# Two layers of long convolution and gated MLP on one core: copies, order of rows, late sums and turned rows in a planned instruction stream

## The chip, the cores and the metric

The kernel runs on one core of a Trainium2 chip. The core has a matrix engine (TensorE, PE in the profile; its weight loads are PEld), a vector engine (VectorE, DVE), an activation engine (ScalarE, ACT), a general engine (GpSimd, POOL) and a queue engine (SyncE, SP) that only issues DMAs here. Each takes its own instructions in order; they wait for one another through semaphores. SBUF is the working memory. PSUM is the small memory into which TensorE writes its products. The metric is the device time of one execution in microseconds; lower is better.

## The reference

All data are bfloat16 with S = 2048 tokens, D = 576 and F = 4608. Two layers with the same weights follow each other, each of them a convolution gate A and an MLP B, both with a residual and a layer norm in front:

```python
kv = k_shift * v                          # k_shift: causal 4-tap filter of k
y  = irfft(rfft(kv) * rfft(ssm_k))[:S]    # convolution of length S along the tokens
y  = y + kv * ssm_D
A(q) = q * y
B(x) = (gelu(x @ w_gate) * (x @ w_up)) @ w_down

x = q
x = x + A(layernorm(x)); x = x + B(layernorm(x))
x = x + A(layernorm(x)); x = x + B(layernorm(x))
```

The convolution's result y depends on k, v and the filter alone, not on x, so both layers use the same y.

## The kernel before

**Tiling.** The 2048 tokens are four chunks c of 512, each four rows j of 128 tokens (RT = 4). A unit is one layer on one chunk; the eight units are, in order, (0,0), (0,1), (1,0), (1,1), (0,2), (0,3), (1,2), (1,3), numbered 0 to 7. They are done in the passes [0], [1,2], [3,4], [5,6], [7]. F is cut into three phases (NP = 3) of 12 column tiles (FP = 12). A visit is one unit in one phase, and within a pass the phases are the outer loop, so that two units share the streamed weights: 24 visits.

**A visit.** For each of 12 column tiles fi, `gu` (L834) makes the gate and the up product in one PSUM slot "gu", 18 matmuls. ScalarE takes the gelu of the gate half (L1317, ga), and VectorE multiplies it with the up half out of PSUM (L1318, hT). Then for each row j 24 matmuls (L1330, dn) make the down product in a slot "dn". VectorE adds it to the residual x_c: L1365 in the first phase, L1367 in the second, L1359 in the third for layer 0, and for layer 1 the third writes the output tile ob (L1350), which a DMA stores. The slots of gu and dn come from `pr` (L607), which goes round three PSUM slots. A fourth slot is that of the convolution, cps. In the down products the convolution may also take a slot of the three (`conv.alt`).

**Rows of a unit.** Before a unit's first visit each of its rows is gated with the convolution (ScalarE yh at L731, VectorE x_c at L741), its mean and variance are found (POOL L692, ScalarE square at L700, POOL L707 and L708), it is normalised to bf16 (VectorE xn at L770 and L772) and turned, so that features lie on partitions, by two DMA transposes issued from SP (`spread`, L798) into xnT. These steps lie in two lists: `vq` for VectorE (in order) and `aq` for ScalarE (by priority). There is one yh tile, four xn tiles and two ob tiles.

**The convolution.** It works by chunks (`Conv.step`): filter kv (VectorE L253, L259, L265), forward products of kv and of the filter (TensorE L285, ScalarE eo at L288, VectorE L293), products of spectra (VectorE L301, L304, L305) summed over chunks in f32 tiles ac (L476), sums and differences (L313, L318), and four inverse products (TensorE L328, ScalarE copy into y at L330). Chunk 0 is done in the prologue (0 to some 50 us). Chunk m = 1 is done beside unit 0's three visits and is needed by unit 1, which follows them. Spectra of earlier chunks are kept in DRAM and come back as kr and hr by DMAs that POOL issues (L391, L395).

**What sets the order.** The program is written out engine by engine in the order in which the Python code emits it. A small model of time, `Pace` (fields pe, dve, act), is advanced by constants (C_GU = 1.944 us for a column tile, C_DN, C_HT and so on). After each tile and within the down products `fill` (L866) is called with a limit: it issues loads that are due, and puts out VectorE work from the convolution (`run_v`) or from the rows (`run_vq`) as long as the model's VectorE stays below the limit, then at most one ScalarE task (`run_aq`), and, where `tensor` is true, up to three pieces of convolution on TensorE (`run_p`). In the up/gate stage the limit lies LEAD = 1.8 us past the next tile, and `tensor` is true while `hurry()` holds, that is until the last inverse product of chunk 1 has been put out. `conv_first` (while chunk 1 has VectorE work left) puts the convolution ahead of the rows. `pressing` says that the unit due next still has rows to make; then the convolution's VectorE work is held back.

Of the kernel before, what the change touches and what calls it, by code (L numbers as in the profile page):

```python
# [18 lines left out]
P = 128  # L19
# [4 lines left out]
HW = 288  # L24
# [11 lines left out]
C_TT, C_ST, C_BN, C_NORM, C_HT, C_GELU, C_EVA, C_EVD, C_YH = 0.76, 0.82, 0.47, 0.62, 0.69, 0.6, 0.66, 0.76, 0.8  # L36
LAG = 0.25
AHEAD = 2.0
HOLD, LEAD = 14.0, 1.8
# [91 lines left out]
class Conv:  # L131
# [9 lines left out]
    def __init__(self, tc, ctx, pace, A_k, A_v, A_shift_k, A_ssm_k, A_ssm_D, ident, cps, ypool):  # L141
        self.tc, self.nc, self.t = tc, tc.nc, pace
        self.k2, self.v2, self.hk = A_k[0], A_v[0], A_ssm_k
        self.S, self.D = self.k2.shape
        self.NB = self.S // BS
        self.KS = A_shift_k.shape[1]
        self.sk, self.sD = A_shift_k, A_ssm_D
        self.ident, self.cps, self.ypool = ident, cps, ypool
        D = self.D
        pool = lambda name, bufs: ctx.enter_context(tc.tile_pool(name=name, bufs=bufs))  # L150
        self.cst = pool("c_cst", 1)
        self.krp = pool("c_kr", 3)
# [17 lines left out]
        self.y_at = {(0, j): 0.0 for j in range(RT)}  # L170
        self.kv_at, self.fwd_at, self.hf_at, self.hd_at = {}, {}, {}, {}
# [149 lines left out]
    def inverse(self, m, mt, terms):  # L321
# [8 lines left out]
        nc.scalar.activation(out=self.halves(self.y[m][:, mt, :]), in_=ps[:, :, 0:HW], func=ACT.Copy)  # L330
# [4 lines left out]
    def store(self, dst, t, ready):  # L335
        self.spills.append((ready, lambda: self.nc.gpsimd.dma_start(out=dst, in_=t[:])))
# [5 lines left out]
    def step(self, m, kv=None, loaded=False):  # L342
# [115 lines left out]
        def v(kt, a, part):  # L458
            def run():
                K = kc[kt] if a == m else kr[(kt, a)][1]  # L460
                if a == 0:
                    acc[kt, part] = self.acp.tile([P, D], F32, tag="ac", name="ac")
                prs[part] = self.prod(part, K, hr[(kt, a)][1], acc[kt, part][:] if a == 0 else None)
# [9 lines left out]
        def more(kt, part):  # L473
            def run():
                into = acc[kt, part][:]
# [12 lines left out]
        def shift(kt, part):  # L488
            def run():
                for sg in range(2):  # L490
                    prev = self.yb[(1 - part, kt, sg)]
                    self.shifted(nyb[part, kt, sg], prev, part)
                    z[(part, kt, sg)] = prev
                return lambda when: mark(("z", kt, part), when + LAG)
            return run
        now = lambda: 0.0
        for kt in KTS:
            order = [(a, part) for a in range(m + 1) for part in range(2)]
            for a, part in order if kt < 2 else sorted(order, key=lambda k: k[1]):
                keys = [("ld", kt, a)] + ([("kc", kt % 2, s, h) for s in range(2) for h in range(2)] if a == m else [])  # L500
                self.V.append((get(*keys), C_P1 if part else C_P0, v(kt, a, part)))
                if a > 0:
                    self.V.append((now, C_AC, more(kt, part)))
# [12 lines left out]
        def inv(mt):  # L516
            def run():
                self.yb = nyb
                self.inverse(m, mt, [(self.lhs(kt, s, mt), z[(s, kt, mt % 2)])
                                     for kt in range(2) for s in range(2)])  # L520
                done = t.on_act(C_EVA, t.pe + 0.98 + LAG)
# [45 lines left out]
def ssm_geglu_kernel(ctx, tc, A_q, A_k, A_v, A_shift_k, A_ssm_k, A_ssm_D, B_x, B_w_gate, B_w_up,  # L567
# [38 lines left out]

    def pr(name):  # L607
        taken[0] += 1
# [7 lines left out]
    gwork = pool("gwork", 1)  # L616
# [5 lines left out]
                lambda: bank(turn[3], "cps"), ypool)  # L622
# [54 lines left out]
    def sum_task(c, j, v):  # L677
# [5 lines left out]
        aq.append((2, lambda: xb_at.get(c, NEVER), C_SQ, run))  # L683
# [12 lines left out]
    def square_task(get_x, v):  # L696
# [14 lines left out]
        aq.append((0 if v["pfx"] == "l_" else 2, at_v(v, "nm_at"), C_SQ, run))  # L711

    def run_aq(limit):
        found = [(prio, n) for n, (prio, ready, cost, run) in enumerate(aq) if ready() <= t.pe]
# [3 lines left out]
        _, _, cost, run = aq[n]  # L718
# [6 lines left out]
    def gate_task(c, j, g):  # L725
        def ready():
            return NEVER if gates[0] is not g else max(conv.y_at.get((c, j), NEVER), g.get("rstd_at", NEVER))
# [6 lines left out]
        aq.append((1, ready, C_YH, run))  # L734
# [19 lines left out]
    def act_early(c):  # L754
        gvars[c] = [{"pfx": "e_"} for _ in range(RT)]
# [7 lines left out]
    def prep(ui, j):  # L763
        layer, c = units[ui]
        v = nvars.setdefault(ui, [{"pfx": "l_"} for _ in range(RT)])

        def norm(j):
            def run():
                xn = xnp.tile([P, XW], BF16, tag="xn", name="xn")
# [3 lines left out]
                xn_made.append((ui, j, xn, t.dve + C_NORM + 0.3))  # L773
# [13 lines left out]
    def g_sum(c, j):  # L787

        v = hvars.setdefault(c, {})[j] = {"pfx": "g_"}
# [3 lines left out]
    xn_made = deque()  # L793

# [14 lines left out]
    def run_vq(limit):  # L809
# [7 lines left out]
        else:  # L817
            r = NEVER if len(xn_made) >= 3 else need[1].get("rstd_at", NEVER)
# [21 lines left out]
    def gu_half(pair, fi, n):  # L840
        gu(pair, wgu[fi // FG], fi % FG, lambda a: a.rearrange("p (j q) -> p j q", q=P)[:, n::2, :], xnT_of[0])

# [18 lines left out]
    def pressing():  # L861

        ui = coming[0]
        return ui is not None and xn_done.get(ui, 0) < RT and (units[ui][1], 0) in conv.y_at and bool(vq)

    def fill(limit, tensor, conv_first):  # L866
        weights()
        conv.run_loads()
        spreads()
        while True:  # L870
            if conv_first:
# [5 lines left out]
        if tensor:  # L877
            for _ in range(3):
                if not conv.run_p():
# [11 lines left out]
    with tc.manual_schedule():  # L891
# [7 lines left out]
        with ExitStack() as es:  # L899
# [257 lines left out]
            for j in (0, 2, 1, 3):  # L1157
# [42 lines left out]
                def norm(j=j):  # L1200
                    v = vs0[j]
                    xn = held["xn", j] = xnp.tile([P, XW], BF16, tag="xn", name="xn")
# [73 lines left out]
        for n, (wb, ph, ui, first, final) in enumerate(visits):  # L1276
            coming[0] = next((v[2] for v in visits[n + 1:] if v[2] != ui), None)
            layer, c = units[ui]
            while xn_done.get(ui, 0) < RT:
                if not run_vq(t.pe + 3.0):  # L1280
                    conv.run_loads()
                    run_aq(t.pe + 3.0)
                    conv.run_v(t.pe + 1.5)
                    conv.run_p()
                    t.pe += 0.2
                spreads()
# [13 lines left out]
            end = ph == NP - 1  # L1300
            hT = hpool.tile([P, FP, CH], BF16, tag="hT", name="hT")
            free = deque([0.0] * 3)
            conv.alt = None
            for fi in range(FP):
# [11 lines left out]
                ga = work.tile([P, CH], F32, tag="ga", name="ga")  # L1316
                nc.scalar.activation(out=ga[:], in_=pair[:, 0, :], func=ACT.Gelu_apprx_tanh)  # L1317
                nc.vector.tensor_tensor(out=hT[:, fi, :], in0=ga[:], in1=pair[:, 1, :], op=ALU.mult)  # L1318
                free.append(t.on_dve(C_HT, t.on_act(C_GELU, t.pe + 0.15) + 0.15) + 0.1)
                if gi == FG - 1 and final:  # L1320
                    when_due(t.pe + (FP - FG) * C_GU + 12.0, load_wgu, n + 3)
                fill(t.pe + C_GU + LEAD, hurry(), conv.left > 0)
            for j in range(RT):
# [24 lines left out]
                if layer == 1 and end:  # L1348
                    ob = work.tile([P, D], BF16, tag="ob", name="ob")
                    nc.vector.tensor_tensor(out=ob[:].rearrange("p (h d) -> p h d", h=2), in0=xh,  # L1350
                                            in1=acc[:, :, 0:HW], op=ALU.add)
                    dst = out2[c * CH:(c + 1) * CH, :].rearrange("(p j) d -> p j d", j=RT)[:, j, :]
                    if wb == NWB - 1:
                        nc.sync.dma_start(out=dst, in_=ob[:])
                    else:
                        conv.store(dst, ob, t.pe + 0.2 + C_EVD + LAG)
                elif end:
                    v = g_sum(c, j)
                    nc.vector.scalar_tensor_tensor(out=xh, in0=acc[:, :, 0:HW], scalar=1.0, in1=xh, op0=ALU.mult,  # L1359
                                                   op1=ALU.add, accum_out=v["s"][:])  # L1360
                    mean_after(v, t.pe + 0.2 + C_EVD + LAG)
                    square_task(lambda xa=xa: xa, v)
                elif ph == 0:
                    m_, op = shift.pop((c, j))
                    nc.vector.scalar_tensor_tensor(out=xh, in0=acc[:, :, 0:HW], scalar=m_[:, 0:1], in1=xh, op0=op, op1=ALU.add)  # L1365
                else:
                    nc.vector.tensor_tensor(out=xh, in0=xh, in1=acc[:, :, 0:HW], op=ALU.add)  # L1367
                t.on_dve(C_EVD, t.pe + 0.2)
                if layer == 0 and end:
                    vq.extend(prep(units.index((1, c)), j))  # L1370
# [51 lines left out]
```

## Time and profile before

The median of three runs is 960.4 us (960.04 to 961.02). The profile is of another execution.

| what | value |
|---|---|
| time of the profiled execution | 961.26 us |
| its span, first to last instruction | 959.5 us |
| mean granted TensorE clock | 0.993 |
| TensorE busy | 931.6 us, 97% |
| VectorE busy | 562.7 us, 59% |
| ScalarE busy | 312.8 us, 33% |
| POOL busy | 139.0 us, 14% |
| gu matmuls, L837 | 561.2 us |
| dn matmuls, L1330 | 292.8 us |
| gelu, L1317, 285 of them | 598 ns each |
| hT, L1318, 285 of them | 686 ns each |
| first term of a sum, f32 (L305, ac<-prod), 24 of them | 758 ns each |
| later terms of it in bf16 (L305, prod<-prod), 48 of them | 458 ns each |

How to read the lines shown later: in the table by stretch each engine has its busy time and, in brackets, its instructions; then follow the granted clock (1.00 is full speed), the mean busy share of the DMA engines and GB/s. A line of the timeline has start, length, engine, line of the program, operation, tile written <- tiles read, shape, count, and in square brackets the idle time of the engine before it with what ended it. In the chain, the steps are those that the end of the program hung on.

### The profile page before, as it was taken

How to read it: one execution, taken by the hardware profiler on the slowest of the kernel's cores; microseconds unless marked ns; L12 is line 12 of the kernel's file. 1: busy time of each engine (PE TensorE's matmuls, PEld its weight loads, DVE VectorE, ACT ScalarE, POOL GpSimd, SP SyncE). 2: the span in 40 equal slices, each digit the busy share in tenths (PEclk: the TensorE clock that was granted, in tenths of full speed). 3: DMA queues.
4: the chain of work that ended last, by engine and by line, in shares of the span. 5: the costliest groups of instructions: out<-in, count | busy, mean ns of one | idle time of the engine just before them, and what ended most of it. 6: DMA issues, size and time to landing. Idle time of an engine off the chain costs nothing.

```text
span 959.5 us, 19259 instructions
## 1 busy us (share of the span) xinstructions
PE 931.6 (97%) x8198; PEld 540.0 (56%) x8198; DVE 562.7 (59%) x1030; ACT 312.8 (33%) x560; POOL 139.0 (14%) x302
## 2 busy tenths in 40 slices
PE   8999999499999999999999999999999999999998
PEld 5756466255646656556466465466466456456455
DVE  7768886367988965677899723543333324423332
ACT  5654214351322335433211521552211214411211
POOL 2214101312211203222020200230000002100000
PEclk9999999799999999999999999999999999999999
DMA  9999986726843722893591540483540540596730
GB/s 236 182 282 266 270 246 120 173 51 177 197 154 120 139 75 83 192 234 76 113 282 40 99 125 14 87 172 78 99 124 1 101 123 11 93 234 148 152 71 25
DMA packets 128970, 131.02 MB, mean 137 GB/s; under 512 B 43378, under 2 KB 121075, under 8 KB 128884
## 3 DMA queue, kind: packets, MB, share of 16 engines
q1 hardware_dynamic: 119554, 93.34, 45.7%
q0 software_dynamic: 9200, 35.54, 11.7%
q8 instruction: 64, 1.05, 0.5%
q10 hardware_dynamic: 130, 0.90, 0.3%
q14 instruction: 22, 0.18, 0.1%
HBM read 108.53 MB, written 11.80 MB: 125 GB/s over the span
## 4 chain that ended last, share of the span: by engine, by line
PE 92%; DMA 2%; issue 2%; DVE 1%; ACT 1%; POOL 0%; SPq 0%; DVEq 0%; ACTq 0%; POOLq 0%
PE gu L837 57%; PE dn L1330 27%; PE cps L285 2%; PE ps L276 2%; PE cps L328 1%; DMA out_dram<-ob 1%; DMA xnT<-xn 1%; PE ps L837 1%; DMA k<-in_A_k_dram 1%; PE ps L1015 1%; PE ps L1121 1%; PE ps L1047 0%; PE ps L1142 0%; ACT yh L731 0%; DVE x_c L741 0%
## 5 line engine op out<-in xcount | busy, mean ns | idle before, releaser
L837 PE MATMUL gu<-xnT,wgu 64*128 64x512 bf16 x5130 | 561.2, 377 | 8.4 <-DMA xnT<-xn 7.4
L837 PEld LDWEIGHTS <-wgu 64*128 64x128 bf16 x5238 | 256.7, 94 | 313.6 <-issue 20.4
L1317 ACT ACTIVATE ga<-gu 128x512 f32<-128x512 f32 x285 | 170.3, 598 | 538.9 <-PE gu L837 535.1
L1318 DVE TENSOR_TENSOR hT<-ga,gu 128x512 bf16<-128x512 f32 x285 | 195.5, 686 | 246.8 <-ACT ga L1317 246.3
L1330 PE MATMUL dn<-wd,hT 128*128 128x288 bf16 x2304 | 292.8, 286 | 0.5 <-DVE ob L1339 0.5
L1330 PEld LDWEIGHTS <-hT 128*128 128x128 bf16 x2304 | 223.5, 98 | 66.5 <-issue 10.5
L1367 DVE TENSOR_TENSOR x_c<-x_c,dn 128x576 f32<-128x576 f32 x32 | 24.1, 753 | 39.1 <-PE dn L1330 38.9
L692 POOL TENSOR_SCALAR means<-s 128x1 f32<-128x1 f32 x28 | 9.4, 336 | 227.7 <-DVE x_c L1359 193.8
L288 ACT ACTIVATE eo<-cps 128x576 f32<-128x576 f32 x48 | 30.5, 649 | 24.4 <-PE cps L285 17.1
L1365 DVE SCALAR_TENSOR_TENSOR x_c<-dn,means,x_c 128x576 f32<-128x576 f32 x28 | 22.8, 815 | 24.8 <-PE dn L1330 24.8
L476 DVE TENSOR_TENSOR ac<-ac,prod 128x576 f32<-128x576 f32 x48 | 36.2, 754 | 0.7
L708 POOL TENSOR_TENSOR rstd<-ve,neghalf_t 128x1 f32<-128x1 f32 x56 | 35.5, 634 | 4.7
L391 POOL DMA_DIRECT2D kr<-Kd x24 | 13.3, 552 | 100.3 <-DVE prod L304 100.3
L1350 DVE TENSOR_TENSOR ob<-x_c,dn 128x576 bf16<-128x576 f32 x15 | 11.3, 753 | 27.9 <-PE dn L1330 19.3
L731 ACT ACTIVATE yh<-y,rstd 128x576 f32<-128x576 bf16 x28 | 21.6, 772 | 14.0 <-DVE x_c L741 11.5
L395 POOL DMA_DIRECT2D hr<-Hd x36 | 19.5, 543 | 45.2 <-DVE prod L304 45.1
L305 DVE TENSOR_TENSOR prod<-prod 128x576 bf16<-128x576 bf16 x48 | 22.0, 458 | 1.7
L1359 DVE SCALAR_TENSOR_TENSOR x_c<-dn,x_c 128x576 f32<-128x576 f32 x16 | 12.1, 757 | 17.5 <-PE dn L1330 16.6
L700 ACT ACTIVATE junk<-x_c,nm 128x576 bf16<-128x576 f32 x28 | 21.5, 768 | 1.3 <-POOL nm L692 1.3
L293 DVE TENSOR_TENSOR kc<-eo 128x288 bf16<-128x288 f32 x48 | 19.3, 453 | 4.2 <-ACT eo L288 3.8
L707 POOL TENSOR_SCALAR ve<-ss 128x1 f32<-128x1 f32 x56 | 15.4, 275 | 38.0 <-ACT junk L700 37.5
L293 DVE TENSOR_TENSOR hh<-eo 128x288 bf16<-128x288 f32 x48 | 19.3, 452 | 2.3 <-ACT eo L288 2.2
(139 smaller groups left out, 539.6 us busy)
## 6 DMA issues: line engine op xcount, KB each, us to landing
wgu<-in_B_w_gate_dram SPq DMA_DIRECT2D x45, 576.0 KB, 5.7
wd<-in_B_w_down_dram SPq DMA_DIRECT2D x30, 864.0 KB, 7.7
wgu<-in_B_w_up_dram SPq DMA_DIRECT2D x45, 512.0 KB, 7.6
hr<-Hd POOLq DMA_DIRECT2D x36, 288.0 KB, 5.6
kr<-Kd POOLq DMA_DIRECT2D x24, 288.0 KB, 5.2
Kd<-kc POOLq DMA_DIRECT2D x12, 288.0 KB, 6.2
Hd<-hh POOLq DMA_DIRECT2D x12, 288.0 KB, 4.2
k<-in_A_k_dram POOLq DMA_DIRECT2D x3, 1008.0 KB, 9.6
```

The lines of the kernel that those rows point to most:

```text
L288: nc.scalar.activation(out=eo[:], in_=ps[:, :, 0:HW], func=ACT.Copy, scale=scale)
L293: self.nc.vector.tensor_tensor(out=dst, in0=eo[:, 0, :], in1=eo[:, 1, :], op=op)
L305: nc.vector.tensor_tensor(out=dst, in0=pr[:, 0, :], in1=pr[:, 1, :], op=ALU.subtract if part == 0 else ALU.add)
L476: nc.vector.tensor_tensor(out=into, in0=into, in1=prs[part], op=ALU.add)
L708: nc.gpsimd.tensor_tensor(out=v["rstd"][:], in0=ve[:], in1=neghalf_t[:, 0:1], op=ALU.pow)
L731: nc.scalar.activation(out=g["yh"][:], in_=conv.y[c][:, j, :], func=ACT.Identity, scale=g["rstd"][:, 0:1], bias=1.0)
L837: nc.tensor.matmul(cols(pair[:, s, :]), lhsT=w[r0:r0 + HK, k, gi * P:(gi + 1) * P], rhs=cols(xnT[r0:r0 + HK, blk_of[k], :]), start=(k == 0 ...
L1317: nc.scalar.activation(out=ga[:], in_=pair[:, 0, :], func=ACT.Gelu_apprx_tanh)
L1318: nc.vector.tensor_tensor(out=hT[:, fi, :], in0=ga[:], in1=pair[:, 1, :], op=ALU.mult)
L1330: nc.tensor.matmul(acc[:, h, 0:HW], lhsT=hT[:, fi, j * P:(j + 1) * P], rhs=wd[2 * wb + fi // WT][:, fi % WT, h * HW:(h + 1) * HW], start=( ...
L1365: nc.vector.scalar_tensor_tensor(out=xh, in0=acc[:, :, 0:HW], scalar=m_[:, 0:1], in1=xh, op0=op, op1=ALU.add)
L1367: nc.vector.tensor_tensor(out=xh, in0=xh, in1=acc[:, :, 0:HW], op=ALU.add)
```

## The change

It has five parts.

- **Copies by ScalarE in the first visits.** While `hurry()` holds, and if the model's ScalarE is not behind, ScalarE takes the gelu into bf16 and then copies the up half out of PSUM into bf16 too, and VectorE multiplies the two from SBUF. The PSUM slot is free after the copy. `fill` may then work FAR = 3.6 us past the next tile.
- **First terms of the convolution's sums stay bf16**, and the second term makes the f32 sum from two bf16 products.
- **Rows of the unit that is due go first.** `pressing` holds from the moment when VectorE has finished the chunk's spectra. While it holds, `run_aq` takes tasks of that unit alone, and TensorE gets no further convolution work once that chunk's y is there. Gating has priority over squares and has two yh tiles. The inverse's copy goes to VectorE if ScalarE is behind it.
- **Down sums put out when ready.** The sum of a down product is not put out right behind it. It goes into a list `late`; `fill` puts it out first thing when the model says that it is ready, and `pr` does at the latest before its slot comes round. Sums that make the output (ob) are put out at once as before. The ob tiles now come from the four xn tiles, in one ring with the rows.
- **Last rows turned by TensorE.** Rows that are finished in the last SLOW = 6 us of the visit before, or are missing when their visit is to begin, are turned by nine TensorE transposes into the cps slot and copied out by VectorE or ScalarE (`turn_row`).

```diff
+SLOW = 6.0
+HOLD, LEAD, FAR = 14.0, 1.8, 3.6
...
-                prs[part] = self.prod(part, K, hr[(kt, a)][1], acc[kt, part][:] if a == 0 else None)
+                prs[part, a] = self.prod(part, K, hr[(kt, a)][1])
...
-                nc.vector.tensor_tensor(out=into, in0=into, in1=prs[part], op=ALU.add)
+                nc.vector.tensor_tensor(out=into, in0=prs[part, 0] if a == 1 else into, in1=prs[part, a], op=ALU.add)
...
+                if max(t.dve, t.pe + 0.98) < max(t.act, t.pe + 0.98):
+                    nc.vector.tensor_copy(out=out, in_=in_)
...
+    def run_late(limit):
+        if not late or late[0][0] > t.pe or max(t.dve, t.pe - 1.0) + C_EVD > limit:
+            return False
+        ready, _, run = late.popleft()
+        run()
+        t.on_dve(C_EVD, ready)
+        return True
...
     def pr(name):
+        while late and taken[0] - late[0][1] >= 2:
+            ready, _, run = late.popleft()
+            run()
+            t.on_dve(C_EVD, ready)
         taken[0] += 1
...
-    gwork = pool("gwork", 1)
+    gwork = pool("gwork", 2)
...
     def run_aq(limit):
-        found = [(prio, n) for n, (prio, ready, cost, run) in enumerate(aq) if ready() <= t.pe]
+        only = coming[0] if pressing() else None
+        found = [(prio, n) for n, (prio, ready, cost, run, ui) in enumerate(aq) if (only is None or ui == only) and ready() <= t.pe]
...
+    ring = deque(maxlen=4)
...
+    def out_tile():
+        if not xn_open():
+            spreads(True)
+            conv.flush(NEVER)
+        return xn_tile()
...
-    def spreads():
-        while xn_made and xn_made[0][3] <= t.pe:
-            ui, j, xn, _ = xn_made.popleft()
+    def spreads(now=False, tensor=False):
+        while xn_made and (now or xn_made[0][3] <= t.pe):
+            if tensor and xn_made[0][0] == ahead[1] and t.pe > ahead[0] - SLOW and conv.ps_free[0] <= t.pe:
+                turn_row(*xn_made.popleft())
+                continue
...
+    def turn_row(ui, j, xn, when, entry):
...
+        pt = conv.cps((P, 2, 1024), BF16)
+        for b in range(NKC):
+            c0 = b * P if b < 5 else HK + (b - 5) * P
+            nc.tensor.transpose(pt[:, b // 8, (b % 8) * P:(b % 8 + 1) * P], xn[:, c0:c0 + P], ident[:])
...
+        if max(t.dve, t.pe) <= max(t.act, t.pe) + 0.3:
+            nc.vector.tensor_copy(out=dst, in_=src)
...
+        else:
+            nc.scalar.copy(out=dst, in_=src)
...
     def pressing():
-        return ui is not None and xn_done.get(ui, 0) < RT and (units[ui][1], 0) in conv.y_at and bool(vq)
+        return ui is not None and xn_done.get(ui, 0) < RT and units[ui][1] in conv.z_at and bool(vq)
...
     def fill(limit, tensor, conv_first):
         weights()
         conv.run_loads()
-        spreads()
+        spreads(tensor=tensor)
         while True:
+            if run_late(limit):
+                continue
...
             for _ in range(3):
-                if not conv.run_p():
+                if pressing() and (units[coming[0]][1], RT - 1) in conv.y_at or not conv.run_p():
                     break
...
             while xn_done.get(ui, 0) < RT:
-                if not run_vq(t.pe + 3.0):
+                if xn_made and xn_made[0][3] - 0.3 <= t.pe:
+                    turn_row(*xn_made.popleft())
+                elif not run_late(t.pe + 3.0) and not run_vq(t.pe + 3.0):
...
-                ga = work.tile([P, CH], F32, tag="ga", name="ga")
-                nc.scalar.activation(out=ga[:], in_=pair[:, 0, :], func=ACT.Gelu_apprx_tanh)
-                nc.vector.tensor_tensor(out=hT[:, fi, :], in0=ga[:], in1=pair[:, 1, :], op=ALU.mult)
-                free.append(t.on_dve(C_HT, t.on_act(C_GELU, t.pe + 0.15) + 0.15) + 0.1)
+                if hurry() and t.act <= t.pe + 0.2:
+                    ga = work.tile([P, 2, CH], BF16, tag="ga", name="ga")
+                    nc.scalar.activation(out=ga[:, 0, :], in_=pair[:, 0, :], func=ACT.Gelu_apprx_tanh)
+                    nc.scalar.copy(out=ga[:, 1, :], in_=pair[:, 1, :])
+                    nc.vector.tensor_tensor(out=hT[:, fi, :], in0=ga[:, 0, :], in1=ga[:, 1, :], op=ALU.mult)
+                    there = t.on_act(2 * C_GELU, max(t.pe + 0.15, gone[0]))
+                    gone.append(t.on_dve(C_HB, there + 0.15) + 0.1)
+                    free.append(there + 0.1)
+                    lead = FAR
+                else:
+                    ga = work.tile([P, CH], F32, tag="ga", name="ga")
+                    nc.scalar.activation(out=ga[:], in_=pair[:, 0, :], func=ACT.Gelu_apprx_tanh)
+                    nc.vector.tensor_tensor(out=hT[:, fi, :], in0=ga[:], in1=pair[:, 1, :], op=ALU.mult)
+                    gone.append(t.on_dve(C_HT, t.on_act(C_GELU, max(t.pe + 0.15, gone[0])) + 0.15) + 0.1)
+                    free.append(gone[-1])
+                    lead = LEAD
...
-                fill(t.pe + C_GU + LEAD, hurry(), conv.left > 0)
+                fill(t.pe + C_GU + lead, hurry(), conv.left > 0)
...
-                    ob = work.tile([P, D], BF16, tag="ob", name="ob")
+                    ob, entry = out_tile()
...
-                elif end:
...
-                t.on_dve(C_EVD, t.pe + 0.2)
...
+                else:
+                    def plus(c=c, j=j, layer=layer, ph=ph, end=end, acc=acc, xa=xa, xh=xh):
...
+                    late.append((t.pe + 0.2, taken[0], plus))
```

More of the change, by code (lines that the diff above doesn't have):

```diff
@@ L329, in inverse, with store, run @@
                                  start=(n == 0), stop=(n == len(terms) - 1))
-        nc.scalar.activation(out=self.halves(self.y[m][:, mt, :]), in_=ps[:, :, 0:HW], func=ACT.Copy)
+        return self.halves(self.y[m][:, mt, :]), ps[:, :, 0:HW]
     def spill(self, dst, t, ready=0.0):
         self.spills.append((ready, lambda: self.nc.gpsimd.dma_start(out=dst, in_=t[:].rearrange("p s d -> p (s d)"))))
-    def store(self, dst, t, ready):
-        self.spills.append((ready, lambda: self.nc.gpsimd.dma_start(out=dst, in_=t[:])))
+    def store(self, dst, t, ready, entry):
+        def run():
+            self.nc.gpsimd.dma_start(out=dst, in_=t[:, 0:self.D])
+            entry[0] = True
+        self.spills.append((ready, run))
     def flush(self, now, keep=0):
@@ L502, in step @@
                 if a > 0:
-                    self.V.append((now, C_AC, more(kt, part)))
+                    self.V.append((now, C_AC, more(kt, part, a)))
                 if kt >= 2 and a == m:
@@ L518, in run @@
                 self.yb = nyb
-                self.inverse(m, mt, [(self.lhs(kt, s, mt), z[(s, kt, mt % 2)])
-                                     for kt in range(2) for s in range(2)])
-                done = t.on_act(C_EVA, t.pe + 0.98 + LAG)
+                out, in_ = self.inverse(m, mt, [(self.lhs(kt, s, mt), z[(s, kt, mt % 2)])
+                                                for kt in range(2) for s in range(2)])
+                if max(t.dve, t.pe + 0.98) < max(t.act, t.pe + 0.98):
+                    nc.vector.tensor_copy(out=out, in_=in_)
+                    done = t.on_dve(C_EVD, t.pe + 0.98 + LAG)
+                else:
+                    nc.scalar.activation(out=out, in_=in_, func=ACT.Copy)
+                    done = t.on_act(C_EVA, t.pe + 0.98 + LAG)
                 self.ps_free[self.cur] = done + LAG
@@ L717, in run_aq @@
         n = min(found)[1]
-        _, _, cost, run = aq[n]
+        cost, run = aq[n][2:4]
         if max(t.act, t.pe - 1.0) + cost > limit:
@@ L754, in act_early @@
     def act_early(c):
-        gvars[c] = [{"pfx": "e_"} for _ in range(RT)]
+        gvars[c] = [{"pfx": "e_", "ui": units.index((0, c))} for _ in range(RT)]
         for j in range(RT):
```

113 lines of the change are left out of this document (75 added, 38 removed).

## The prediction

> **What bounds the kernel now.** I read the page first, then the chain of work in order of time, the table by stretch, the waits, and last the timeline around single places.
>
> ```profile
> span 959.5 us, 19259 instructions
> PE 931.6 (97%) x8198; PEld 540.0 (56%) x8198; DVE 562.7 (59%) x1030; ACT 312.8 (33%) x560; POOL 139.0 (14%) x302
> ```
>
> TensorE is busy for 931.6 of 959.5 us, so only the 27.9 us in which it stands, and its slow clock, can be won; work taken off another engine counts only where TensorE waits for it. The chain in order of time (start, length, what) shows where that is:
>
> ```profile
> 131.04 23.42 PE gu L837 x216
> ...
> 178.57 1.27 SPq L798
> 179.93 7.11 DMA xnT<-xn
> 187.08 25.87 PE gu L837 x216
> ```
>
> An undisturbed visit has 23.42 us of up/gate products (12 groups of 1.952) and 11.87 us of down products. The visit at 187.08, the first of unit 1, starts only when the last rows of its input, turned by DMA, have landed, and its products take 25.87 us. The table by stretch (length, then busy time by engine, then granted clock) gives the size of the hole and what leads to it:
>
> ```profile
> 98.40:156.50 58.10, 58.10 (x524) 30.59 (x519) 52.74 (x93) 13.80 (x24) 3.74 (x7) 1.00 0.89 226
> 172.10:187.10 15.00, 2.74 (x18) 1.53 (x16) 6.78 (x20) 6.84 (x14) 6.82 (x14) 0.70 0.77 164
> 187.10:213.00 25.90, 25.90 (x217) 12.83 (x217) 13.40 (x29) 11.04 (x22) 3.83 (x11) 0.91 0.45 105
> ```
>
> From 98.4 to 156.5 VectorE is busy 52.74 of 58.10 us with the convolution of chunk 1; then come its inverse products (157.5), the rows of unit 1, and the hole: 2.74 us of TensorE work in 15.00 us, clock 0.70, then 0.91. ScalarE has 13.80 of 58.10 us in use. The waits (who for whom: total, times, longest) name the rest:
>
> ```profile
> PE gu L837 <- DMA xnT<-xn: 7.4, 1, 7.4
> PE cps L285 <- ACT eo L288: 5.2, 3, 2.5
> PE gu L837 <- DVE ob L1350: 1.0, 1, 1.0
> ```
>
> 4.8 us of the 5.2 lie inside the hole (gaps of 2.3 and 2.5 us before 175.34 and 178.52). The third line is small, but it tells of the PSUM ring, and so does an ordinary boundary in the timeline:
>
> ```profile
> 671.83 6.43 PE L837 MATMUL gu<-xnT,wgu 64*128 64x512 bf16 x58
> 671.93 0.82 DVE L1365 SCALAR_TENSOR_TENSOR x_c<-dn,means,x_c 128x576 f32<-128x576 f32 x1 [2.12 <-PE dn L1330]
> 673.98 0.60 ACT L1317 ACTIVATE ga<-gu 128x512 f32<-128x512 f32 x1 [13.32 <-PE gu L837]
> 674.61 0.69 DVE L1318 TENSOR_TENSOR hT<-ga,gu 128x512 bf16<-128x512 f32 x1 [1.86 <-ACT ga L1317]
> ...
> 852.49 0.75 DVE L1350 TENSOR_TENSOR ob<-x_c,dn 128x576 bf16<-128x576 f32 x1 [2.69 <-DMA out_dram<-ob]
> ...
> 853.30 4.92 PE L837 MATMUL gu<-xnT,wgu 64*128 64x512 bf16 x44 [1.00 <-DVE ob L1350]
> ```
>
> At 853.30 the third group of a visit waited for the last down sum of the visit before: the sum ended at 853.24 (852.49 + 0.75), the products went on 0.06 later. Three PSUM slots go round, so the third group needs the slot of the last down row.
>
> **The change, part by part.** Sums are against the profiled execution's own time, 961.26 us (span 959.5); the median is 960.4, 0.9 less.
>
> *The hole (gain).* Of its 15.00 us four convolution groups of 0.49 us (L285) must be done anyway: 15.0 - 1.96 = 13.0 us. The slow clock costs 25.87 - 23.42 = 2.45 more. Full gain: 15.5 us. Whether it goes depends on when chunk 1 is ready. From 98.4 to 156.5 VectorE does 24 products hT at 0.684 us. With both operands copied down as bf16, I price one by the nearest row, 0.458 us for a 576-wide bf16 product with bf16 output; scaled to 512, 0.41. 24 x 0.27 = 6.6 us. The first term of each sum now stays bf16: 8 x (0.758 - 0.458) = 2.4 us. VectorE stood 5.4 us in this stretch, nearly all (5.7 by that line's idle time) before products waiting for ScalarE; with 3.6 us of work allowed ahead instead of 1.8 I take half away, 2.7. So 156.5 becomes about 145, even if the stretch starts no earlier. Before, it took 2.3 us to the first y copy (158.77) and 20.2 from there to the last xn row (178.36 + 0.57); at the same pace that row is there at about 167.5, while TensorE is busy until about 171. Rows of the due unit go first now, so the pace should be better. By DMA the fourth row landed 8 us after its xn (187.08), which would be 175.5; on TensorE it takes 0.56 + 0.76 us (next item), 169. Between no gain (rows as late as before) and 15.5 us it is nearest to the latter: I take 15.5.
>
> The cover for this is ScalarE: a copy of about 0.60 us (the gelu row, same shape) in each of up to 36 groups, 21.6 us. In 98.4 to 156.5 that raises 13.8 by 14.4 to 28 of 58 us. Each group then holds ScalarE 1.2 of 1.952 us, so the copies are hidden; in the first visit, with convolution copies of 0.65 and sums of 0.87 to 0.96 between them, ScalarE's clock in the planner passes over some. Without that cover each late copy would cost TensorE up to 0.6 us.
>
> *Turned rows (loss).* One row is 9 transposes. In the prologue a set of 8 plus 2 halves took about 0.56 us of TensorE (first matmul 50.24, next set 50.81), the copy 0.76 on VectorE or 1.12 on ScalarE, hidden where the row is not the last. Only rows finished in the last 6 us of a visit, or missing at its start, go this way. Before, only unit 1 is that late: unit 3's transposes ended 16 us before use, unit 7's 11 us. Bounds 0 and 4 x 0.6 = 2.4 us; I take one row, 0.6. SP loses their DMA issues (1.26 us each, two a row), which frees weight loads behind them.
>
> The Trainium skill, TensorE: Matmul & The Clock Gate, Part 4, gives about 275 ns per 128x128 transpose in a kernel, which would make a row 9 x 0.275 = 2.5 us by that estimate, and the sum 1.9 us worse. The trace disagrees: ten of them in 0.56 us.
>
> *Down sums put out later (loss).* This is the part that speaks against the change. Before, the sum of the last row of a visit went to VectorE at once (671.93). Now it is queued and put out in the next fill, which comes only after the next visit's first group has its products, gelu and hT product in the queues. So on VectorE it stands behind hT. From the lines above: hT ends at 675.30 (the next instruction starts 0.08 earlier), the sum takes 0.82 (first phase) or 0.75, so it ends at 676.04 or 675.97, and the third group, due at 671.83 + 2 x 1.952 = 675.73, starts at 676.10 or 676.03: 0.37 or 0.30 us lost. 24 visits, less 4 that end with a store (sum still at once, the last visit among them), leave 20 such boundaries. Two lie in the first visits, where the gelu is followed by the copy: product ends 0.6 - 0.27 later, loss about 0.65 each. Of the other 18, 7 are first phases: 7 x 0.37 + 11 x 0.30 + 2 x 0.65 = 7.2 us. Bounds: 0 (if a slot is free after all) and 18 x 2.3 (below); the 853.30 line shows that the slot is needed, so 7.2. For the other three rows of a visit the next fill comes 0.245 us later with nothing put between: nothing, as long as VectorE isn't planned further ahead than 0.74 us; then it is put off by a down step or two, and the slot is needed only three takes later.
>
> *3.6 us ahead (loss).* At the end of a visit in the copying stage, the last hT product may stand behind 3.6 us of other work, while the down products reach it after 11 x 0.245 = 2.7 us. Bounds 0 and 2 x 1.4 us; after the second visit VectorE is full, I take 0.9.
>
> *Stores from the ring of four xn tiles (gain).* The 1.00 us at 853.30 (1.16 against the undisturbed pace) came from ob waiting for a store to land, with two tiles. With four it waits for transposes of unit 7, done 840. Gain 1.1. POOL still issues the stores, in order behind the convolution's loads as before.
>
> *Two gate tiles; the inverse's copy on VectorE when ScalarE is behind; no convolution products on TensorE while due rows press.* These move work whose deadlines are far: chunk 2's inverse ran at 334, its rows are due at 456; chunk 3's at 551, due at 637. Zero, covered by those 86 to 122 us; without that cover each visit's delay is TensorE idle one for one. The short waits of cps for a sum (2.3 us in total outside the hole) I leave as they are; between 0 and twice that.
>
> Sum: 961.3 - 15.5 - 1.1 + 0.6 + 7.2 + 0.9 = 953.4 us profiled, less 0.9 for the median: **952.5**.
>
> **Rivals.**
> 1. *The late sums cost nothing,* because sums go ahead of hT or a slot is free: 952.5 - 7.2 = 945.3. Against it: the order in the loop, and 853.30. Chance 0.12.
> 2. *The rows are still late,* by chunk 1's kr and hr loads (8.5 us to land between 97 and 123, with DMA near 1.00 busy) or a last row by DMA: half the hole, 7.4 us, stays: 959.9. For it: DMA is full until 132. Against: no VectorE wait for a kr or hr load is listed. Chance 0.09.
> 3. *Slower: the late sum slips behind the second group's hT.* Then it ends 1.95 us later, and each of 18 boundaries costs 2.3 instead of 0.33: 952.5 + 35 = 988. It decides as soon as a boundary costs over 0.75 us ((15.5 + 1.1 - 0.6 - 0.9) / 20). It needs VectorE planned over 3 us ahead at the boundary; late visits are too idle for that (VectorE under half busy). Chance 0.05.
> 4. *ScalarE becomes the bound in the copying stage:* 0.4 us in each of 24 groups, 9.6 us: 962.1. Against it: 1.2 of 1.952 us. Chance 0.09, half of it on the slower side.
> 5. *Transposes let the clock fall:* as after the hole, 2.45 us: 955. In the stretch 48.0 to 98.4, which holds 20 of them, the granted clock is 1.00. Chance 0.03. The Trainium skill, same page and part, says that transposes do not count as busy for the clock gate; by it this rival would come true whenever several rows are turned in a row.
>
> **How the numbers follow.** The forecast has 0.62, its own range 949 to 956. A difference under 0.2% (1.9 us) can't be told from none here. Faster (under 958.5): the forecast, rivals 1 and 5, and 0.04 of the rest: 0.81. Same: most of rival 2 and a little of 4: 0.09. Slower: rivals 3, half of 4, a piece of 2: 0.10. Range 945 to 960: it takes in rivals 1 and 2.
>
> **What would show it.** After: no DMA wait of gu at unit 1's start, clock 1.00 throughout; hT in two forms, one near 0.41 us; gu waiting for x_c about 20 times at 0.3 to 0.7 us, all at the third group of a visit; no wait for ob. The prediction is wrong if these x_c waits are absent or over 0.75 us each, if a wait on ScalarE's ga or copies shows in the first three visits, or if xnT is still awaited.

## The result and the profile after

The changed kernel has a median of 954.88 us (954.69 to 959.04, nine runs) against 960.4 us before: a ratio of 0.9946, 95% interval 0.9934 to 0.9957. It is faster by 5.5 us. The profiled execution has 954.88 us, against 961.26 before.

The head of its page, and from the table by stretch the same first window as before (length, busy time by engine, clock, DMA share, GB/s):

```profile
span 953.1 us, 19333 instructions
PE 933.3 (98%) x8225; PEld 536.5 (56%) x8225; DVE 550.0 (58%) x1034; ACT 326.2 (34%) x590; POOL 136.2 (14%) x302
...
PEclk9999999999999999999999999999999999999999
```

```profile
98.40:156.50 58.10, 57.33 (x515) 29.45 (x512) 45.35 (x93) 25.02 (x47) 3.79 (x7) 1.00 1.00 241
156.00:174.20 18.20, 17.35 (x159) 14.11 (x158) 11.38 (x27) 8.93 (x17) 6.56 (x16) 1.00 0.45 88
```

TensorE now stands about 20 us of the span instead of 28, and its granted clock is 1.00 over this execution (0.993 before). ScalarE carries 25.0 us where it carried 13.8, VectorE 45.4 where it carried 52.7. In the second window, which ends with the start of unit 1, TensorE works 17.35 of 18.20 us: of the hole one wait of 0.85 us is left. The chain in order of time shows this, and below it an ordinary pair of visits:

```profile
170.14 2.69 PE dn L1426 x22
173.38 0.77 DVE xnT L910
174.19 2.13 PE gu L889 x18
176.41 0.60 ACT ga L1410
177.03 0.69 DVE hT L1411
177.72 0.69 DVE x_c L1460 x2
178.46 19.60 PE gu L889 x180
...
290.91 2.07 PE gu L889 x18
293.00 0.60 ACT ga L1410
293.63 0.69 DVE hT L1411
294.32 0.67 DVE x_c L1468
295.04 19.60 PE gu L889 x180
314.64 11.87 PE dn L1426 x96
326.51 2.07 PE gu L889 x18
```

Unit 1 starts at 174.19 instead of 187.08, released by VectorE's copy of a row that TensorE turned (L910). And the chain now leaves TensorE at the start of 20 up/gate stages, all but the first and the three that follow a visit that ends with a store: after one group it runs over gelu, hT and the last down sum (x_c) before the third group may start. A visit takes 326.51 - 290.91 = 35.60 us, where it took 707.18 - 671.89 = 35.29 in the chain before. Both were forecast, the second as the loss that speaks against the change.

### The profile page after: what moved, and what is told of

The parts are those of the page before. It is cut to its first block, busy times and chain, and to the rows that moved or that the text cites. A ratio compares the mean times of both kernels' runs of the same rounds, so it can differ in the third digit from the quotient of the medians.

```text
span 953.1 us, 19333 instructions
## 1 busy us (share of the span) xinstructions
PE 933.3 (98%) x8225; PEld 536.5 (56%) x8225; DVE 550.0 (58%) x1034; ACT 326.2 (34%) x590; POOL 136.2 (14%) x302
## 4 chain that ended last, share of the span: by engine, by line
PE 87%; DVE 5%; DMA 5%; ACT 2%; issue 1%; SPq 0%; ACTq 0%; DVEq 0%
PE gu L889 55%; PE dn L1426 28%; DMA nat<-in_A_ssm_k_dram 2%; PE cps L288 2%; DVE hT L1411 1%; ACT ga L1410 1%; PE cps L331 1%; DMA wgu<-in_B_w_gate_dram 1%; DVE x_c L1466 1%; DMA Hd<-hh 1%; PE ps L889 1%; DMA k<-in_A_k_dram 1%; DVE x_c L1468 1%; PE ps L1092 0%; DVE x_c L1460 0%
## 5 line engine op out<-in xcount | busy, mean ns | idle before, releaser
L889 PEld LDWEIGHTS <-wgu 64*128 64x128 bf16 x5238 | 251.8, 94 | 315.3 <-issue 8.2
L1411 DVE TENSOR_TENSOR hT<-ga,gu 128x512 bf16<-128x512 f32 x256 | 175.7, 686 | 252.8 <-ACT ga L1410 251.5
L1410 ACT ACTIVATE ga<-gu 128x512 f32<-128x512 f32 x256 | 152.8, 597 | 491.1 <-PE gu L889 485.1
L291 ACT ACTIVATE eo<-cps 128x576 f32<-128x576 f32 x48 | 30.9, 651 | 26.9 <-PE cps L288 14.9
L308 DVE TENSOR_TENSOR prod<-prod 128x576 bf16<-128x576 bf16 x72 | 33.0, 458 | 2.5
L1401 ACT ACTIVATE ga<-gu 128x512 bf16<-128x512 f32 x29 | 17.3, 597 | 44.5 <-PE gu L889 41.2
L401 POOL DMA_DIRECT2D hr<-Hd x36 | 19.4, 541 | 45.4 <-DVE prod L307 45.4
L1403 DVE TENSOR_TENSOR hT<-ga 128x512 bf16<-128x512 bf16 x31 | 13.0, 421 | 20.8 <-ACT ga L1402 20.8
L1447 DVE TENSOR_TENSOR xn<-x_c,dn 128x576 bf16<-128x576 f32 x15 | 11.3, 753 | 23.0 <-PE dn L1426 23.0
L721 POOL TENSOR_SCALAR nm<-s 128x1 f32<-128x1 f32 x28 | 8.6, 308 | 90.0 <-DVE x_c L773 89.9
```

Of the source, the lines that this page charges most:

```text
L291: nc.scalar.activation(out=eo[:], in_=ps[:, :, 0:HW], func=ACT.Copy, scale=scale)
L308: nc.vector.tensor_tensor(out=dst, in0=pr[:, 0, :], in1=pr[:, 1, :], op=ALU.subtract if part == 0 else ALU.add)
L721: nc.gpsimd.tensor_scalar(out=v["nm"][:], in0=v["s"][:], scalar1=-1.0 / D, scalar2=None, op0=ALU.mult)
L889: nc.tensor.matmul(cols(pair[:, s, :]), lhsT=w[r0:r0 + HK, k, gi * P:(gi + 1) * P], rhs=cols(xnT[r0:r0 + HK, blk_of[k], :]), start=(k == 0 ...
```

## The experiments

None of the twelve kernels leaves out a part of the work. "Spectra" are the last differences yb of chunk 1 (L318 before, L321 after); "last xn" is the end of the normalisation (L770 before, L802 after) of unit 1's last row. The three times are those of the profiled execution. The experiments were run in several rounds, in which the kernel before had medians of 959.8 to 960.5 us, so differences below 1 us between rows of the table are not told apart.

| kernel | median us | spectra done | last xn done | unit 1 starts |
|---|---|---|---|---|
| before | 960.4 | 156.6 | 178.9 | 187.1 |
| changed | 954.9 | 152.8 | 172.1 | 174.2 |
| 1: changed, last sum at once | 947.8 | 150.6 | 171.3 | 173.0 |
| 7: as 1, no copies | 951.6 | 155.9 | 174.1 | 176.2 |
| 11: as 1, rows by DMA | 954.6 | 150.8 | 170.6 | 178.0 |
| 12: as 1, no copies, rows by DMA | 954.4 | 156.6 | 171.6 | 178.8 |
| 6: as 1, copies from the second visit | 948.6 | 146.6 | 171.1 | 174.3 |
| 9: as 6, copies until the spectra | 946.1 | 147.2 | 170.3 | 172.6 |

**1. The last sum at once.**

```diff
                     late.append((t.pe + 0.2, taken[0], plus))
+                    while j == RT - 1 and late:
+                        late.popleft()[2]()
+                        t.on_dve(C_EVD, t.pe + 0.2)
```

> The changed kernel, but the sum of the last down row of a visit goes to VectorE at once, ahead of the next visit's first hT; all other sums stay late. Theory (the third group of a visit waits for that sum's PSUM slot, 0.31 to 0.59 us at each of 20 boundaries, 7.4 us in all): about 954.9 - 7.4 = 947.5 us, and no visit's up/gate stage over 23.5 us outside the first three visits. Rival (the longer up/gate stages come from the two late hT products themselves, not from the slot): 954.9, stages stay at 23.7 to 23.8 us.

947.76 us: 7.1 us less than the changed kernel, ratio 0.9867 (0.9853 to 0.9882) to the kernel before. Every up/gate stage from the fifth visit on is back at 23.42 us, and no wait of gu for x_c is left in the list of waits. In the chain, the stage that began at 290.91 above is one piece again:

```profile
288.93 23.42 PE gu L889 x216
```

The theory holds; the slot is what costs.

**2. Rows by DMA.**

```diff
-            if tensor and xn_made[0][0] == ahead[1] and t.pe > ahead[0] - SLOW and conv.ps_free[0] <= t.pe:
-                turn_row(*xn_made.popleft())
-                continue
...
-                if xn_made and xn_made[0][3] - 0.3 <= t.pe:
-                    turn_row(*xn_made.popleft())
-                elif not run_late(t.pe + 3.0) and not run_vq(t.pe + 3.0):
+                spreads()
+                if not run_late(t.pe + 3.0) and not run_vq(t.pe + 3.0):
```

> The changed kernel, but no row is turned by TensorE: the last rows of unit 1 go through DMA transposes too, as in the kernel before. Theory 1 (the turning closes the rest of the hole; the rows are made only 6.6 us earlier than before, and a DMA-turned row lands 8 us after its xn): the first visit of unit 1 starts at about 172.3 + 8 = 180 instead of 174.2, less 2 us of transposes saved, and the clock falls for part of it: 959 to 962 us. Theory 2 (order of rows and faster VectorE close the hole by themselves): 953 to 955 us.

964.04 us, 9.2 more than the changed kernel and slower than before (ratio 1.0046, 1.0028 to 1.0064). Theory 1 holds in kind, but the time lies above its range. Its profiled execution, the longest of the six with 968.35 us, shows two things that add to it. A late sum cost 2.1 us at one place, as in experiment 3. The other stands in the first visit, where the program is the same as the changed kernel's. From the timelines of VectorE, first the changed kernel, then this one:

```profile
87.27 0.46 DVE L296 TENSOR_TENSOR kc<-eo 128x288 bf16<-128x288 f32 x1 [0.79 <-DMA Hd<-hh]
```

```profile
90.77 0.46 DVE L296 TENSOR_TENSOR kc<-eo 128x288 bf16<-128x288 f32 x1 [3.53 <-DMA Hd<-hh]
```

VectorE waits for the store of a filter spectrum hh, whose tile kc takes over: 0.8 us in one execution, 3.5 in another, and TensorE's next convolution group waits 0.9 and 3.6 us for the down sum that stands behind it in VectorE's queue. The kernel before has no such wait.

**3. No copies.**

```diff
-                if hurry() and t.act <= t.pe + 0.2:
+                if False:
```

> The changed kernel without ScalarE's copies of up and without the wider limit of 3.6 us: every hT reads PSUM, as before. Theory of the prediction (the copies bring chunk 1's spectra forward by about 9 us): y of chunk 1 comes 6 us or more later than in the changed kernel, and the visit of unit 1 starts 4 to 8 us later: 959 to 963 us. Rival (the start of the products is set by the loads of kr and hr, which came 11 us later behind the stores in POOL's queue, so the copies bought nothing): within 2 us of 954.9 either way.

963.1 us, as the prediction's theory has it. But not all of the 8.2 us is the copies' doing. In the second visit one group stood 2.15 us, where the changed kernel's third group stands 0.42:

```profile
98.46 0.81 DVE L1466 SCALAR_TENSOR_TENSOR x_c<-dn,mv,x_c 128x576 f32<-128x576 f32 x1
...
99.33 1.62 PEld L889 LDWEIGHTS <-wgu 64*128 64x128 bf16 x18 [2.64 <-DVE x_c L1466]
99.33 1.90 PE L889 MATMUL gu<-xnT,wgu 64*128 64x512 bf16 x16 [2.15 <-DVE x_c L1466]
```

Here the late sum stops the second group already. This fits the convolution having taken a slot of the ring in the last down row, so that the ring comes round one group sooner: here a convolution group stands at 93.26 in the timeline, inside that row, while in the changed kernel the last 44 recorded down products of the visit run without one. The slots themselves don't show in the trace, and it was not tried by itself. Experiment 7 takes the late sums out.

**4. Copies and bf16 first terms alone**, added to the kernel before.

> The kernel before with the relief of VectorE alone: ScalarE's copies of up in the first visits with the 3.6 us limit, and the first terms of the sums in bf16. Sums at once, rows in the old order, all rows by DMA. Theory of the prediction (VectorE's time is what makes chunk 1 late): y some 9 us earlier, the hole of 15.5 us shrinks by as much: 950 to 953 us. Rival (loads behind stores in POOL's queue set the start of the products): y at most 2 us earlier, 958 to 961 us.

959.22 us (957.6 to 964.7, ten runs), ratio 0.9994 (0.9974 to 1.0014): no gain that can be told. The spectra were done at 150.8, some 6 us earlier than before, and unit 1 started at 177.1, ten us sooner. But unit 1's first visit gave back 4.0 us in its up/gate stage (29.77 instead of 25.81): it had waited 4.3 us for a DMA turn before its first product and waited another 3.0 for the next turn right behind it. It gave back 4.3 more in its down stage, 2.0 of it convolution work that had run in the hole. Neither theory fits: VectorE did get earlier, and the time did not follow.

**5. Turning alone**, added to the kernel before.

> The kernel before with TensorE's turning of rows alone: rows that are finished in the last 6 us of the visit before, or missing at its start, are turned by TensorE; sums at once, rows in the old order, no copies. In the kernel before the fourth xn was there at 179.15 and its DMA turn landed at 187.08. Theory (the DMA turn of the last rows is 7 us of the hole, and without idle time over 7 us the clock stays up): unit 1 starts at about 181, 5 to 7 us earlier, and 2 us of clock come on top: 952 to 955 us. Rival (without the copies the rows are so late that turning alone wins little): 957 to 960 us.

960.41 us, ratio 1.0004 (0.9995 to 1.0013). My theory fell; it is as the rival says. In the old order the last xn was done only at 181.1, and the turned rows' ScalarE copies stood behind its other work: TensorE waited 3.3 and 3.2 us for them.

**7, 11 and 12: what each part is worth, sums at once.** 7 has the edits of 1 and 3, 11 those of 1 and 2, 12 all three.

> Last sum at once, and no copies at all. Theory (the copies bring the spectra forward by about 8 us, and what the rows cannot make good again is idle TensorE): 952 to 955 us, against 947.8 with copies. Rival (the loss of 8 us without copies came mostly of late sums colliding with a fuller VectorE): 948 to 950 us.

> Last sum at once, copies, rows of the due unit first, but every row turned by DMA. In the first experiment the last xn was there at 171.4 and unit 1 started at 173.0. Theory (with the rows early enough, turning by TensorE is worth the DMA's latency, some 8 us less 2 us of transposes, and the clock with it): 954 to 957 us. Rival (the 9 us that the second experiment lost came from a late sum or a late store in the first visit): 948 to 950 us.

> Last sum at once, no copies, every row turned by DMA: of the change there remain the order of the rows, the sums inside a visit put out when ready, the bf16 first terms and the ring of xn tiles. Theory (order, copies and turning each move the same chain, and only what is left of the hole can be won): 957 to 959.5 us, some 2 us better than before from the ring and the order. Rival (the order is the main part of the gain): 952 to 955 us.

| | rows by DMA | rows by TensorE |
|---|---|---|
| no copies | 954.4 | 951.6 |
| copies | 954.6 | 947.8 |

In 11 the theory is right, in 12 the rival: the order of the rows with the ring and the small parts is the largest piece, 6.0 us (0.9935, 0.9912 to 0.9957). They were not taken apart further; the ring alone is worth 1.2 us (below). In 12 the spectra are as late as before, yet the last xn comes 7.3 us sooner. What is left is the DMA's latency; of the waits of experiment 12:

```profile
PE gu L886 <- DMA xnT<-xn: 7.5, 1, 7.5
```

By the medians, turning by TensorE takes 2.8 us of that without copies and 6.8 with them; copies are worth nothing with DMA turns and 3.8 us with TensorE's. Experiment 11 scatters: four of its ten runs took 958.6 to 963.2 us, the other six 953.8 to 954.7. So copies with DMA turns may well be worth less than nothing. For 7, 951.6 lies just below the theory's range: about half of what experiment 3 lost was the late sums.

**6, 8, 9 and 10: can the copies bring more?** The products of spectra started at 104.24, 5 us later than before, since POOL issued the first load of kr later. POOL's timeline, the kernel before and the changed one:

```profile
82.31 0.61 POOL L391 DMA_DIRECT2D kr<-Kd  x1
```

```profile
92.36 1.07 POOL L336 DMA_DIRECT2D Kd<-kc  x2 [4.88 <-DVE kc L296]
93.42 0.55 POOL L397 DMA_DIRECT2D kr<-Kd  x1
```

Experiment 6 makes the copies only with `wb > 0`, 8 counts the loads as possible 3 us after the last filter spectrum, 9 adds `1 not in conv.z_at` to 6, and 10 adds it to 1 (the copies end with the spectra).

> Last sum at once as in the first experiment, and ScalarE's copies only from the second visit on. Theory (in the first visit the copies hold up ScalarE's convolution copies, so the filter's store comes later, POOL issues the kr and hr loads behind it at 93.4 instead of 82.3, and the products start 5 us later): loads at about 82, first product at about 99, spectra done about 4 us earlier than with copies throughout; unit 1 starts without a wait: 945 to 947 us. Rival (the copies are worth as much in the first visit as later): 949 to 951 us.

> Last sum at once, copies throughout, and one constant changed: the loads of chunk 1's kr and hr count as possible 3 us after the last filter spectrum instead of 10 us, so POOL issues them ahead of the stores of kc. Theory (the loads' place behind those stores is what delays the products): first product at 97 to 100 instead of 104, spectra done some 4 us earlier: 945 to 947 us. Rival (the loads then wait in POOL's queue for the filter's store to land and hold up the stores of kc, which gives the time back): 947 to 950 us.

> Last sum at once, ScalarE's copies from the second visit on, and only until VectorE has finished chunk 1's spectra (before: until the last inverse product). With copies from the second visit on, the spectra were done at 146.6, yet the last xn came at 171.1, with VectorE busy 3.8 of 11.2 us in between. Theory (between spectra and rows ScalarE, holding 1.2 us of each group for copies, leaves no room for the gates, one task a group): the rows come 2 to 4 us sooner, fewer of them are turned by TensorE, unit 1 starts without a wait: 946 to 947.5 us. Rival (one inverse product a group through the one cps slot sets the pace): rows no sooner, 948.5.

> Last sum at once, copies from the first visit on, but only until the spectra are done. The spectra then come at about 150, three groups before the end of the third visit's up/gate stage. Theory of ScalarE's room: up to 1 us better than 947.8, since only three groups lose their copies. Rival (pace of the inverses): 947.8.

6: 948.59 us. Loads at 81.7, first product at 98.7, spectra 4 us sooner than in experiment 1, all as the theory has it, and still no gain (0.8 us more by the median): the last xn does not move (171.1). Without copies, in experiment 3, the loads are at 81.7 and the first product at 99.2 too. So the loads' place in POOL's queue does delay the spectra, but the spectra are no longer what unit 1 waits for. 8: 947.0 us (945.98 to 952.39), not clearly different from experiment 1; in its profiled execution, the 952.39, POOL waited 4.8 us for the filter's store. 9: 946.06 us, ratio 0.9855 (0.9843 to 0.9868), the lowest time here. Its interval is clear of experiment 10's, from the same round (0.9871 to 0.9907), but overlaps those of 1 and 6 (0.9864 to 0.9894), so that it is faster than these two is not shown. Its time fits the theory, its cause only in part: the rows came 0.8 us sooner, not 2 to 4; three instead of four were turned, and no turned row's copy fell to ScalarE, for which TensorE had waited 1.2 us in 6. 10: 947.9 us, as its rival says.

What pins the last xn at 170 to 172 was not separated further: between the spectra and the rows lie four inverse products, one a group through one slot, and eight ScalarE tasks. The timelines show one more candidate. In experiment 9 ScalarE had the gated y of the fourth row (the second of these two yh) at 161.18, and VectorE took it up only at 165.28, behind the copy of a turned row that itself waited for TensorE:

```profile
159.75 1.43 ACT L763 ACTIVATE yh<-y,rstd 128x576 f32<-128x576 bf16 x2
```

```profile
164.61 0.76 DVE L910 COPY xnT<-cps 128x1152 bf16<-128x1152 bf16 x1 [0.91 <-PE cps L905]
165.28 0.81 DVE L773 SCALAR_TENSOR_TENSOR x_c<-x_b,means,yh 128x576 f32<-128x576 bf16 x1
```

The same stands in the changed kernel (164.13 and 167.35) and in experiments 1, 6 and 10, behind such a copy or a late down sum. No run takes it away, so what it costs is open.

## Why the prediction was right or wrong

The forecast was 952.5 us, range 945 to 960; measured 954.9, 2.4 us above. In the profiled execution the change is 954.88 - 961.26 = -6.4 us, against -7.9 forecast, so 1.5 us fell short. The other 0.9 us is the step from the profiled execution to the median: the profiled execution lies 0.9 us above the median before and at the median after.

- **The late sums: right in place, cause and size.** Forecast 7.2 us. From the starts of the stages, 20 boundaries cost 7 x 0.31 + 11 x 0.37 + 0.59 + 0.53 = 7.4 us, and undoing them gave 7.1. Only which sums cost more was wrong: the third phase of layer 0 costs 0.37 like the first. The wait shown before each of the 20 products is only 0.14 to 0.42 us; the list of waits names 13 of them, since the seven of 0.14 us are too short for it:

```profile
PE gu L889 <- DVE x_c L1466: 1.8, 8, 0.4
...
PE gu L889 <- DVE x_c L1460: 0.8, 4, 0.2
```

- **The stores' ring: right.** The first visit of unit 7 has 23.42 us of up/gate products instead of 24.59: 1.2, forecast 1.1. No wait for ob is left.
- **3.6 us ahead: wrong.** Forecast 0.9; the down products show no such gap in the first three visits. It is luck that this 0.9 us, which did not come, makes up for the turned rows.
- **Turned rows: mis-sized.** I took one row; three were turned, at 0.51 us each (165.30, where the nine start, to 165.80, where the next down product does): 1.5, not 0.6. The clock stayed at 1.00. The group of them in the changed kernel:

```profile
L905 PE MATMUL cps<-ident,xn 128*128 128x128 bf16 x27 | 2.0, 219 | 0.0
```

The 219 ns is the time that the trace shows for one; nine in a row hold TensorE for 0.51 us. The Trainium skill's 275 ns (TensorE: Matmul & The Clock Gate, Part 4) is nearer the first number than what a row costs by the second, 0.51 / 9 = 0.057 us each. No run here shows its statement there that transposes don't count as busy for the clock, since the three sets of nine stood apart, between matmuls.

- **The hole: nearly all of it went, but not as forecast.** Of the 15.5 us, 0.85 stayed as the wait for L910. The step that failed is "156.5 becomes about 145": the spectra were done at 152.8. The stretch from first product to last spectrum did shrink, from 57.5 to 48.5 us (a saving of 9.0 against 11.7 forecast; a bf16 hT took 0.421 us against the 0.41 taken). But "even if the stretch starts no earlier" left out that it could start later: 104.24 instead of 99.08, by the loads in POOL's queue. And "at the same pace", 20.2 us from the first y to the last xn, was wrong the other way: it took 14.9 (157.17 to 172.11). Experiment 12, with the spectra as late as before and the last xn 7.3 us sooner, points to the new order, in which the rows of the due unit go first. The second error makes good about half of the first: the first y came 9.9 us later than the forecast's 147.3, the last xn 4.6 later, 172.1 instead of 167.5. That unit 1 started all the same with one short wait is in part luck. The lateness moved the last rows into the end of the visit, which is why three of them were turned, and the turning covered it (experiment 11: 6.8 us more without it).
- **The sum.** 7.4 - 1.2 - (15.5 - 1.5 - 0.85) = -6.95 us. Waits of convolution groups outside the hole grew from 3.2 to 3.9 us (TensorE's gaps before them; the prediction's 2.3 us for those that wait for a sum is 2.8 in the trace), which makes -6.2 against the -6.4 measured. That this fits so closely is partly chance: in the profiled execution the first up/gate products also begin 0.8 us earlier than before (47.38, 48.16 before), so about 0.6 us of loss is not assigned.
- **The rivals.** Rival 1 fell with experiment 1: the late sums cost 7.1 us. Rival 3's price was seen at one boundary each in experiments 3 (2.15 us) and 2 (2.1 us), not at all 20; what fits there is another cause than the one I gave, the convolution's turn in the ring, which was only argued. Rivals 4 and 5 did not come: no wait of gu for ga or a copy is listed, and the clock stayed at 1.00. Rival 2's waits for DMA came true where TensorE's turning was taken out.

## What to carry to other kernels

When a sum is put off in an in-order queue, look for what stands in front of it when it is put out, and which slot it holds: 0.3 us at 20 boundaries ate more than half of what was won at one place. Price a chain to its last link: copies or turning alone gave nothing that could be told, the order of the rows with the ring and the small parts 6.0 us, all of it together 12.7 (960.5 to 947.8 with the last sums at once). Making an engine faster ahead of the chain did nothing here while another link had the last word (experiments 4 and 6). A step moved by a planner moves its loads too; read the queue that issues them before taking a start time as given.

## What the runs showed of the hardware

Nine TensorE transposes held TensorE for 0.51 us, although each shows 219 ns. By DMA, the turn of the last row landed 8 us after the row was there (178.93 to 187.08 before). The same stretch of program waited 0.79 us in one execution and 3.53 in another for a 288 KB store to land; from 78 to 92 us the mean busy share of the DMA engines was 0.73 in the first and 1.10 in the second. And the idle time shown before a waiting product understates the wait: 0.14 or 0.20 us shown, 0.31 or 0.37 us from start to start.
